# A sorted graph aggregation: other bucket counts per part, and merges and gathers begun at other times

## The chip, the core and the metric

One core of a Trainium2 chip runs the kernel. The metric is the device time of one execution in microseconds (us); the median of three runs of the kernel before was 1865.99 (1864.18 to 1870.74). The engines are named as in the profile: PE (matrix multiplication; PEld are its weight loads), DVE (vectors), ACT (activations and copies), POOL (here mostly the issue of indirect DMAs), SP (issue of other DMAs).

## What is computed

One layer of GraphSAGE on 12,500 nodes with 64 features and 800,000 random edges: features of the source nodes are summed for each destination node, scaled, and combined with the node's own features.

```
N, deg, D = 12500, 64, 64
E = N * deg
nsum = segment_sum(x[src], dst, N)       # 800,000 rows of 64 numbers, summed into 12,500
h_neigh = nsum * deg_inv[:, None]
return x @ w_self + h_neigh @ w_neigh
```

## The kernel before

The kernel never gathers the 800,000 rows. It sorts the edges into 7,546 buckets, one for each pair of 164 destination nodes and 128 source nodes, and turns each bucket into two small matrix products with one-hot matrices.

**Keys and sort (lines 249 to 284 and 427 to 464).** Each edge becomes one 32-bit key that holds bucket, half of the bucket, and the positions of source and destination. The keys stand in 128 partitions with 6,250 each. `sort_runs` sorts every partition by compare-exchange stages, a minimum and a maximum on DVE each; elements without a partner are copied by ACT. The last 30 stages are cut at `CUT` into three portions, so that the first part of the sorted run is done before the others.

**Parts, rows, runs.** The buckets are dealt to three parts. Part p has 128 rows with `KPRS[p]` buckets each (29, 20, 10), so part 0 holds buckets 0 to 3,711, part 1 the next 2,560, part 2 the rest. For each part a first gather (`find_rows`, `gather_runs`, lines 516 to 541) brings 16 pieces of the 128 sorted runs into each partition; DVE merges them to one (`merge_runs` over `LENA`, "first pass"); `split_rows` (543 to 570) stores the result, counts where rows begin, and gathers again, 8 pieces for each row; a second pass over `LENB` merges these to one sorted row a partition. `LENS` holds the lengths that are kept in each round. A round (`merge_round`, 300 to 334) begins with a minimum and a maximum (line 316), goes on with levels of the same kind (line 328), and lets ACT copy the elements that a level doesn't touch (line 312); the second level waits for that copy. The last round of part 0 (`merge_last`, 337 to 367) finishes the lower 1,770 elements of a row (`LOWER`) before the upper ones.

**Buckets.** `find_buckets` or `find_and_gather` count where each bucket's middle stands in its row, and a third gather by POOL brings a window of 200 elements a bucket into `v`. `decode_buckets` (766 to 855) splits the keys, four buckets a group: source positions go as bf16 to `sl` in DRAM, destination positions are transposed into `dlT`. What lies beyond the window's 128 elements is a leftover: found by MAX8 operations (857 to 863), collected by `leftovers` (865 to 922; `GRP` rows share one list), and later added by a matrix product of its own, from feature rows gathered by POOL into `lx` (`pick`, 989 to 1000; `HELD` = 5 buffers) and a one-hot (`spread`, line 1006).

**Node stage (`nodes`, 943 to 1090).** 944 tiles of eight buckets. For every 28 buckets SP loads their `sl` rows, spread over all partitions, into `slb` (line 933), and DVE makes the one-hots `ohs` (935) and `ohd` (940). PE multiplies the features by `ohs` into PSUM (966), ACT copies the result to `xg` (976; once the last part is decoded, DVE takes some of these, line 974), and PE multiplies `xg` by `ohd` and sums (1047). After every six destination blocks `finish` writes 984 nodes.

**What sets the order.** Everything from the end of the sort on is issued in an order written out by hand (`after_sort`, `sums_and_merge`, lines 1209 to 1385). The generators yield after each step: merges yield an estimate of their own DVE time in ns, side jobs yield the number of tiles to wait. Ahead of the node stage part 0 goes through alone; part 1's first pass (`merge`) fills in where part 0 waits: up to `WAIT` ns behind part 0's second gather, beside the counts, up to `BEHIND` ns, and beside the decode (1304 to 1309). In the node stage each tile adds `PACE[...] - spent` ns to a budget `t`, and merges are issued while it is positive; the first value of `PACE` that counts is for the time when part 1 is merged, the second for the time after. Part 1's second gather is a side job (`split`); its last yield is followed by the second pass of part 1, with part 2's first pass running meanwhile, and so on to part 2. A part's counts, gathers and decode (`change`, 1279) run one step a tile.

**Queues.** An engine takes its instructions in the order given, and so do the DMA queues of SP and POOL: a leftover gather on POOL whose buffer is still in use holds up the stores and gathers behind it.

Of the kernel before, what the change touches and what calls it, by code (L numbers as in the profile page):

```python
# [31 lines left out]
PITCH1 = 6400  # L32
KPRS = (29, 20, 10)
NP = len(KPRS)
# [6 lines left out]
NCNT = [(k + 3) // 4 for k in KPRS]  # L41
LENS = ((56, 92, 156, 280, 504, 936, 1776, 3424),
        (44, 72, 120, 208, 368, 676, 1264, 2412),
        (32, 48, 72, 124, 204, 368, 676, 1264))
SUP = 8
COUNTED = 4600
WAIT = 20e3
EARLY = 11e3
NSUP = 128 // SUP
LENA = [l[3:] for l in LENS]  # L50
LENB = [l[4:] for l in LENS]
PACE = (0, 420, 405)
LROW = [l[-1] for l in LENS]
LEAD = 616
EXT = 36
SIDE = H + EXT
PITCH2 = [l + 2 * SIDE for l in LROW]
PCS = (19, 13, 9)
PCSN = 14
PIECES = (12, 4)  # L60
GRP = (2, 4, 7)
CHK = [-(-128 // g) for g in GRP]
# [6 lines left out]
SIGMA = 6.0  # L69
LOWER = 1770  # L70
BEHIND = 5e3
NEARLY = 24
LAG = 4
HELD = 5
OCT = 6
OCTM = 256 // OCT + 1
# [223 lines left out]
def merge_round(nc, src, oth, off, other, rstride, nruns, ln, lout, late, filler=()):  # L300
# [18 lines left out]
    for j, (k, lo, *ends) in enumerate(plan):  # L319
        if not j and not late():  # L320
            both()
        for op, end, z in zip((OP.min, OP.max), ends, (1, 2 * k)):
            n = end - lo
# [7 lines left out]
            yield n2 * n / 0.96 + 125  # L331
        if not j:
            yield from islice(filler, 2)
        cur, nxt = nxt, cur


def merge_last(nc, src, oth, off, rstride, ln, lout, split, done):

# [10 lines left out]
    for a, e in alone:  # L349
        z = 2 * (a % ln) + a // ln  # L350
        nc.scalar.activation(at(src, z, e - a), at(oth, z, e - a), AF.Copy)
    edge = [split]
    for (first, *_), (then, *_) in zip(plan[-2::-1], plan[:0:-1]):
# [20 lines left out]
class Kernel:  # L374
# [168 lines left out]
    def split_rows(self, part, u, to, mps, queue):  # L543
# [20 lines left out]
        for j in range(SUP):  # L564
# [4 lines left out]
            yield 1  # L569
        yield 5  # L570

    def merge_runs(self, lens, u, pong, nruns, last=False):

# [5 lines left out]
        for ln, lout in zip(lens, lens[1:]):  # L579
            src, oth = bufs[par], bufs[1 - par]  # L580
            if last and nruns == 2:
                def done(rows):
                    assert rows is u
                    self.lower = True
                yield from merge_last(nc, src, oth, 0, rs, ln, lout, LOWER, done)
            else:
                for dt in merge_round(nc, src, oth, 0, 0, rs, nruns, ln, lout, lambda: self.late):
                    self.hold = dt < 0
                    yield abs(dt)
# [275 lines left out]
    def leftovers(self, part):  # L865
# [11 lines left out]
        for b in range(grp):  # L877
            nc.gpsimd.dma_start(many[:len(range(b, 128, grp)), b, :cand], found[b::grp])
        yield 8
        many = many.rearrange("p b i -> p (b i)")  # L880
# [62 lines left out]
    def nodes(self, pool, aps, mps):  # L943
# [6 lines left out]
        late = []  # L950
        done = []
        acc = None

# [35 lines left out]
        def pick(b0):  # L989
            if self.picked == len(done) or len([u for u in uses if u[5]]) >= HELD:  # L990
                return
# [19 lines left out]
        def add(u, stop=False):  # L1011
            o, _, _, f, e = u[:5]
            n = slice((f - o * OCT) * HN, (e - o * OCT) * HN)
            for h in range(2):
                nc.tensor.matmul(acc[h][:, n], u[5], u[7][:, h, n], start=False, stop=stop)  # L1015
# [193 lines left out]
    def after_sort(self, es, mps, aps):  # L1209
# [7 lines left out]
        with tc.manual_schedule():  # L1217
# [27 lines left out]
            rows = self.find_rows(2, mps)  # L1245
            for _ in self.merge_runs(LENA[0], u0, w0, NSUP):
                if rows and not self.hold and next(rows, None) is None:
# [5 lines left out]
            assert not rows  # L1253
            merge = self.merge_runs(LENA[1], u1, x, NSUP)
            t = 0
# [10 lines left out]
            n = t = 0  # L1266
            for dt in self.merge_runs(LENB[0], w0, u0, SUP, True):
                if self.lower:
# [18 lines left out]
    def sums_and_merge(self, es, mps, aps, x, u1, u2, u3, runs, first_two, va, vp, counts, merge):  # L1287
# [18 lines left out]
        for i, k in enumerate(self.decode_buckets(0, self.v, vp, mps)):  # L1306
            t += 1400 if i < 4 else 2800
            if k < KPRS[0]:
                t = fill(t) if t > 0 else t
        va.close()  # L1310
        first_two.close()
# [101 lines left out]
```

## Time and profile before

| What | Value |
|---|---|
| median of three runs | 1865.99 us |
| profiled execution, its own time | 1856.37 us |
| its span, first to last instruction | 1854.6 us |
| sort done, merges of part 0 begin | 437.6 us |
| second gather of part 0, second pass begins | 583 us, 605.7 us |
| first one-hots of the node stage | 803.4 us |
| first count of part 1, of part 2 | 1173 us, 1575 us |
| busy: DVE, ACT, PE, POOL | 93%, 60%, 53%, 31% |
| moved by DMA | 307.8 MB, 164 GB/s over the span |

The times are microseconds from the start of the span. A line of the timeline gives start, duration, engine, line, operation, written and read tiles, a count where several are put together, and in brackets how long the engine had stood idle and on what. In lines of groups the idle time and its causes stand behind the second bar. "f32 x2 ... 5.00" is two operations that took 5.00 us together. A matmul of line 966 is one bucket, so eight of them are a tile.

### The profile page before, as it was taken

What the parts mean: (1) busy time and instruction counts of PE and PEld (TensorE: products, weight loads), DVE (VectorE), ACT (ScalarE), POOL (GpSimd) and SP (SyncE); (2) the same over time, 40 slices, a digit from 0 to 9 for tenths busy, and PEclk for the clock granted to TensorE, in tenths of its full rate; (3) what the DMA queues carried; (4) which work ended last, traced back from release to release, by engine and by line L of the source; (5) the groups of instructions that cost most, each with busy time, mean ns of one, the idle gap of its engine ahead of it and who ended that gap; (6) DMA issues with size and microseconds to landing.
All of it is one profiled execution on the core that took longest, in us unless ns stands there. A gap on an engine that the chain in (4) does not pass through costs nothing.

```text
span 1854.6 us, 54153 instructions
## 1 busy us (share of the span) xinstructions
PE 986.6 (53%) x23413; PEld 851.9 (46%) x23413; DVE 1718.2 (93%) x1718; ACT 1116.7 (60%) x1587; POOL 576.2 (31%) x447
## 2 busy tenths in 40 slices
PE   3046000000000000058979979897898899888996
PEld 1015000000000000057868868776887788777885
DVE  6999999999999999989989999998898799978885
ACT  5263000113001005458979989899999899977885
POOL 2000000055502005404456535473332523532331
PEclk7567555555555555579989999999999999999998
DMA  5207100021002002169978888996889788977894
GB/s 174 54 0 169 39 0 0 38 79 51 18 4 73 10 0 82 47 216 266 274 249 253 251 248 254 296 282 227 264 250 284 234 265 242 326 200 257 274 268 118
DMA packets 176789, 307.79 MB, mean 166 GB/s; under 512 B 127885, under 2 KB 133596, under 8 KB 175772
## 3 DMA queue, kind: packets, MB, share of 16 engines
q1 hardware_dynamic: 98268, 275.58, 44.9%
q0 software_dynamic: 78272, 28.65, 9.6%
q8 instruction: 185, 3.03, 0.7%
q14 instruction: 64, 0.52, 0.1%
HBM read 277.01 MB, written 26.52 MB: 164 GB/s over the span
## 4 chain that ended last, share of the span: by engine, by line
DVE 19%; PE 13%; DMA 11%; issue 10%; SPq 5%; POOL 4%; ACT 4%; DVEq 0%; POOLq 0%; ACTq 0%
DMA slb<-sl 10%; PE ct L966 7%; DVE u L328 7%; PE acc L1047 5%; SPq L933 5%; DVE ohs L935 4%; DVE ohd L940 3%; ACT xg L976 2%; DVE u L362 2%; POOL u L565 1%; POOL lx L997 1%; POOL out L1123 1%; DVE u L316 1%; DMA sl<-l 1%; PE acc L1015 1%
## 5 line engine op out<-in xcount | busy, mean ns | idle before, releaser
L976 ACT ACTIVATE xg<-ct 128x1024 f16<-128x1024 f32 x919 | 862.6, 1074 | 104.4 <-PE ct L966 80.0
L966 PE MATMUL ct<-xh,ohs 128*128 128x128 f16 x7546 | 532.6, 224 | 87.9 <-DVE ohs L935 23.7
L966 PEld LDWEIGHTS <-ohs 128*128 128x128 f16 x7546 | 451.8, 100 | 125.4 <-issue 52.5
L328 DVE TENSOR_TENSOR u<-u 128x1512 f32<-128x1512 f32 (+57 forms) x316 | 425.7, 1362 | 12.9 <-ACT u L312 8.6
L1047 PE MATMUL acc<-ohd,xg 64*128 64x82 f16 x15092 | 395.2, 201 | 47.7 <-ACT xg L976 20.4
L1047 PEld LDWEIGHTS <-xg 64*128 64x128 f16 x15092 | 324.6, 96 | 104.6 <-issue 29.2
L997 POOL DMA_INDIRECT lx<-xt,ls x127 | 232.0, 1826 | 425.6 <-PE acc L1015 352.5
L940 DVE TENSOR_TENSOR ohd<-iota,dlT 128x2296 f16<-128x2296 bf16 x270 | 362.2, 1341 | 0.0
L935 DVE TENSOR_SCALAR ohs<-slb,pidx 128x3584 f16<-128x3584 bf16 x270 | 321.8, 1192 | 40.2 <-DMA slb<-sl 19.0
L509 PE MATMUL stp<-cx,swapa 128*128 128x16 f32 (+1 forms) x12 | 3.1, 335 | 398.0 <-DVE swapa L505 398.0
L260 DVE TENSOR_TENSOR a<-b 128x1040 f32<-128x1040 f32 (+41 forms) x130 | 194.7, 1539 | 3.5 <-DVE b L260 0.5
L260 DVE TENSOR_TENSOR b<-a 128x1040 f32<-128x1040 f32 (+46 forms) x150 | 194.6, 1345 | 3.2 <-ACT a L262 0.4
L538 POOL DMA_INDIRECT u<-d,ixa x48 | 72.5, 1511 | 390.8 <-ACT junka L526 335.4
L509 PEld LDWEIGHTS stp<-cx,swapa 128*128 128x128 f32 x12 | 2.6, 271 | 398.5 <-DVE swapa L505 398.5
L312 ACT ACTIVATE u<-u 128x256 f32<-128x256 f32 (+14 forms) x60 | 33.0, 618 | 170.6 <-DVE u L316 134.8
L1123 POOL DMA_DIRECT2D out<-o x27 | 99.1, 3800 | 103.1 <-ACT o L1117 89.8
L802 PE MATMUL tr<-idb,l 128*128 128x128 bf16 x59 | 7.6, 263 | 188.9 <-ACT l L796 188.9
L262 ACT ACTIVATE b<-a 128x2 f32<-128x2 f32 (+31 forms) x41 | 15.9, 402 | 127.1 <-DVE a L260 120.4
L802 PEld LDWEIGHTS <-l 128*128 128x128 bf16 x59 | 4.3, 114 | 191.2 <-ACT l L796 190.8
L316 DVE TENSOR_TENSOR u<-u 128x2016 f32<-128x2016 f32 (+11 forms) x40 | 61.9, 1563 | 16.2 <-DMA u<-da,ixb 8.8
L262 ACT ACTIVATE a<-b 128x1 f32<-128x1 f32 (+24 forms) x34 | 8.6, 259 | 105.4 <-DVE b L260 99.9
L565 POOL DMA_INDIRECT u<-da,ixb x24 | 36.9, 1539 | 88.6 <-ACT ixb L513 85.0
(158 smaller groups left out, 839.4 us busy)
## 6 DMA issues: line engine op xcount, KB each, us to landing
slb<-sl SPq DMA_DIRECT2D x1076, 224.0 KB
xt<-xh SPq DMA_DIRECT2D x1, 3136.0 KB
out<-o POOLq DMA_DIRECT2D x25, 123.0 KB
own<-os SPq DMA_DIRECT2D x12, 256.0 KB
out<-os SPq DMA_DIRECT2D x12, 256.0 KB
rd<-dst SPq DMA_DIRECT2D x5, 512.0 KB
rs<-src SPq DMA_DIRECT2D x5, 512.0 KB
lx<-xt,ls POOLq DMA_INDIRECT x127
```

The costliest lines, as they stand in the source:

```text
L260: nc.vector.tensor_tensor(view(dst, lo + sh, [[st, g], [1, l]]), x, y, op=op)
L316: nc.vector.tensor_tensor(at(oth, to, n), x, y, op=op)
L328: nc.vector.tensor_tensor(to, at(cur, ln + lo, n), at(cur, lo + k, n), op=op)
L538: nc.gpsimd.indirect_dma_start(out=u[:, i * w:(i + 1) * w], out_offset=None, in_=src, in_offset=bass.IndirectOffsetOnAxis(ap=self.start[pa ...
L933: nc.sync.dma_start(b[j::4], bass.AP(tensor=src.tensor, offset=src.offset, ap=[[0, 32], [1, n * 128]]))
L935: nc.vector.tensor_scalar(s.rearrange("p c s -> p (c s)"), b, self.pidx[:, :1], None, op0=OP.is_equal)
L940: nc.vector.tensor_tensor(d, self.iota[:, None].to_broadcast(wide), ix, op=OP.is_equal)
L966: nc.tensor.matmul(ct[:, i * 128:(i + 1) * 128], cols[i][0], self.xh[:, (b0 + i) % NB].rearrange("p a f -> p (a f)"), start=True, stop=True)
L976: nc.scalar.activation(xg[:, :cnt * 128], ct[:, :cnt * 128], AF.Copy)
L997: nc.gpsimd.indirect_dma_start(out=x, out_offset=None, in_=self.xt, in_offset=bass.IndirectOffsetOnAxis(ap=self.left[p][1][:, c:c + 1].bit ...
L1047: nc.tensor.matmul(acc[h][:, db % OCT * HN:(db % OCT + 1) * HN], xg[r, i * 128:(i + 1) * 128], d[r], start=db % OCT == 0 and sb == 0, stop ...
L1123: nc.gpsimd.dma_start(out, o[:n, at], accum_op=OP.add)
```

## The change

- The parts get 31, 20 and 8 buckets a row instead of 29, 20 and 10. `LENS` of parts 0 and 2, `LOWER`, the number of MAX8 pieces (`PCS`) and the rows that share a leftover list (`GRP` of part 2: 9 instead of 7) follow. Part 0 then ends at bucket 3,968, part 1 at 6,528.
- Part 1's first pass is handed to the merges of part 0 as a filler: in the rounds of the first pass from length 536 on, in all rounds of the second pass and in `merge_last`, one of its operations is issued between the first min/max pair and the second level. (Before, `filler` was there but empty.)
- `WAIT` is 22e3 instead of 20e3; after the decode of part 0 another 5e3 ns of part 1's merge are issued (`FIRST`).
- `PACE` is 328 and 362 instead of 420 and 405.
- The last yield of `split_rows` is 10 instead of 5: the merge behind a second gather begins five tiles later. The same for the wait of `leftovers` behind its copies: 10 instead of 8.
- `pick` counts a buffer as held for six tiles (`BACK`) after the product that reads it was issued.

```diff
-KPRS = (29, 20, 10)
+KPRS = (31, 20, 8)
-LENS = ((56, 92, 156, 280, 504, 936, 1776, 3424),
+LENS = ((60, 100, 168, 292, 536, 996, 1892, 3648),
         (44, 72, 120, 208, 368, 676, 1264, 2412),
-        (32, 48, 72, 124, 204, 368, 676, 1264))
+        (32, 44, 64, 108, 172, 308, 556, 1032))
-WAIT = 20e3
+WAIT = 22e3
-PACE = (0, 420, 405)
+PACE = (0, 328, 362)
-PCS = (19, 13, 9)
+PCS = (20, 13, 8)
-GRP = (2, 4, 7)
+GRP = (2, 4, 9)
-LOWER = 1770
+LOWER = 1890
+FIRST = 5e3
+BACK = 6
...
@@ merge_round @@
     for j, (k, lo, *ends) in enumerate(plan):
         if not j and not late():
             both()
+            yield from islice(filler, 1)
...
-        if not j:
-            yield from islice(filler, 2)
...
-def merge_last(nc, src, oth, off, rstride, ln, lout, split, done):
+def merge_last(nc, src, oth, off, rstride, ln, lout, split, done, filler=()):
...
         nc.scalar.activation(at(src, z, e - a), at(oth, z, e - a), AF.Copy)
+    yield from islice(filler, 1)
...
@@ split_rows @@
-        yield 5
+        yield 10
-    def merge_runs(self, lens, u, pong, nruns, last=False):
+    def merge_runs(self, lens, u, pong, nruns, last=False, filler=(), since=0):
...
-                for dt in merge_round(nc, src, oth, 0, 0, rs, nruns, ln, lout, lambda: self.late):
+                for dt in merge_round(nc, src, oth, 0, 0, rs, nruns, ln, lout, lambda: self.late,
+                                      filler if ln >= since else ()):
...
@@ leftovers @@
-        yield 8
+        yield 10
...
@@ nodes @@
+        added = []
...
-            if self.picked == len(done) or len([u for u in uses if u[5]]) >= HELD:
+            held = len([u for u in uses if u[5]]) + len([n for n in added if n > len(done) - BACK])
+            if self.picked == len(done) or held >= HELD:
                 return
...
@@ add @@
             o, _, _, f, e = u[:5]
+            added.append(len(done))
...
-            for _ in self.merge_runs(LENA[0], u0, w0, NSUP):
+            merge = self.merge_runs(LENA[1], u1, x, NSUP)
+            for _ in self.merge_runs(LENA[0], u0, w0, NSUP, filler=merge, since=LENA[0][1]):
...
-            merge = self.merge_runs(LENA[1], u1, x, NSUP)
...
-            for dt in self.merge_runs(LENB[0], w0, u0, SUP, True):
+            for dt in self.merge_runs(LENB[0], w0, u0, SUP, True, merge):
...
@@ sums_and_merge, after the decode of part 0 @@
+        fill(FIRST)
         va.close()
```

More of the change, by code (lines that the diff above doesn't have):

```diff
@@ L584, in done @@
                     self.lower = True
-                yield from merge_last(nc, src, oth, 0, rs, ln, lout, LOWER, done)
+                yield from merge_last(nc, src, oth, 0, rs, ln, lout, LOWER, done, filler)
             else:
-                for dt in merge_round(nc, src, oth, 0, 0, rs, nruns, ln, lout, lambda: self.late):
+                for dt in merge_round(nc, src, oth, 0, 0, rs, nruns, ln, lout, lambda: self.late,
+                                      filler if ln >= since else ()):
                     self.hold = dt < 0
```

## The prediction

> **What bounds the kernel now.** I read the page's totals first, then the busy time by stage, the rate of tiles, the waits, and last the timeline at each wait. The columns of the stage tables are stretch, length, then busy us (instructions) of PE, weight loads, DVE, ACT, POOL, then granted clock, DMA share, GB/s; the last four rows are the matmuls of line 966 alone.
>
> ```profile
> span 1854.6 us, 54153 instructions
> PE 986.6 (53%) x23413; PEld 851.9 (46%) x23413; DVE 1718.2 (93%) x1718; ACT 1116.7 (60%) x1587; POOL 576.2 (31%) x447
> 803.00:1633.00 830.00, 727.71 (x18284) 642.41 (x18285) 776.42 (x930) 764.86 (x990) 361.00 (x205) 0.96 0.86 262
> 953.00:1250.00 297.00, 262.79 (x6633) 231.79 (x6634) 291.93 (x314) 271.05 (x344) 152.16 (x70) 0.97 0.87 262
> 1350.00:1428.00 78.00, 70.05 (x1809) 61.76 (x1807) 75.11 (x83) 76.56 (x105) 25.86 (x11) 1.00 0.86 263
> 1633.00:1830.00 197.00, 174.48 (x4618) 157.74 (x4615) 173.98 (x208) 158.82 (x186) 56.92 (x34) 0.97 0.84 252
> 803.00:1170.00 367.00, 188.97 (x2639) 159.16 (x2640) 0.95 0.87 258
> 803.00:1575.00 772.00, 397.12 (x5581) 335.16 (x5582) 0.96 0.86 260
> 953.00:1250.00 297.00, 153.15 (x2167) 128.91 (x2168) 0.97 0.87 262
> 1350.00:1428.00 78.00, 41.27 (x601) 34.66 (x599) 1.00 0.86 263
> ```
>
> Up to 803 us (sorting, then merging and decoding part 0) DVE works almost alone; after it, the node stage runs 944 tiles of eight buckets, and DVE makes their one-hots and merges parts 1 and 2 between them. DVE's 93% is therefore two things. Before 803 every DVE microsecond is a microsecond of the kernel. In the node stage four limits stand close together. From 953 to 1250 DVE is at 291.93/297 = 98% and 2167/8 = 271 tiles take 1.096 us each: DVE's own work is 1.078 a tile, ACT's 271.05/271 = 1.00. From 1350 to 1428 DVE is at 96% and ACT at 98%: 75 tiles, 1.038 each. So taking work off DVE speeds a tile from 1.096 to about 1.04, and there ACT takes over. That is the number on which most hangs.
>
> ```profile
> DVE u L316 <- DMA u<-da,ixb: 8.8, 2, 7.3
> DVE u L328 <- ACT u L312: 8.6, 7, 2.6
> DVE u L316 <- DMA lx<-xt,ls: 7.0, 1, 7.0
> DVE ltop L860 <- DMA many<-top: 2.1, 2, 1.8
> POOL lx L997 <- PE acc L1015: 352.5, 74, 13.2
> 515.42 31.38 DVE L328 TENSOR_TENSOR u<-u 128x1282 f32<-128x1282 f32 x16 [1.64 <-ACT u L312]
> 605.70 4.42 DVE L316 TENSOR_TENSOR u<-u 128x2016 f32<-128x2016 f32 x2 [1.52 <-DMA u<-da,ixb]
> 612.68 31.20 DVE L328 TENSOR_TENSOR u<-u 128x836 f32<-128x836 f32 x16 [2.56 <-ACT u L312]
> 803.41 1.15 DVE L935 TENSOR_SCALAR ohs<-slb,pidx 128x3584 f16<-128x3584 bf16 x1 [6.22 <-DMA slb<-sl]
> 952.74 1.69 DVE L316 TENSOR_TENSOR u<-u 128x1472 f32<-128x1472 f32 x1 [7.25 <-DMA u<-da,ixb]
> 1456.61 1.93 DVE L316 TENSOR_TENSOR u<-u 128x816 f32<-128x816 f32 x2 [6.97 <-DMA lx<-xt,ls]
> ```
>
> A wait of DVE stands in brackets. These are the pauses that the edits touch: the copies of ACT inside merge rounds, the first one-hots after the decode, and the first merges behind the second gathers of parts 1 and 2 (952.74 and 1456.61; the second is put down to a leftover gather, the last thing on POOL's queue then).
>
> **The change part by part.** *Merges.* I wrote out the operations of merge_plan for both tables. All merges together have 453,028 elements a partition before and 453,500 after, with the same 376 operations: DVE saves nothing in sum. They move. Part 0 goes from 220,692 to 235,716 (+15,024), part 2 from 78,504 to 63,952 (-14,552). The price comes from two rows:
>
> ```profile
> 437.64 5.00 DVE L316 TENSOR_TENSOR u<-u 128x2240 f32<-128x2240 f32 x2
> 785.75 1.48 DVE L316 TENSOR_TENSOR u<-u 128x1264 f32<-128x1264 f32 x1
> 583.03 3.69 DVE L316 TENSOR_TENSOR u<-u 128x1664 f32<-128x1664 f32 x2
> 588.00 16.17 DVE L328 TENSOR_TENSOR u<-u 128x936 f32<-128x936 f32 x10
> ```
>
> (5.00/2 - 1.48)/(2240 - 1264) = 1.045 ns an element. Part 0's merges cost +15.7 us ahead of the node stage, uncovered; part 2's cost 15.2 us less inside it. The sort's portions shift by some 7 us of work from the last to the first, their sum stays.
>
> *Fillers.* Six merges of part 1 are put into part 0's later rounds, three in the first pass, three in the second: two of 3.69/2 = 1.85, one near 1.1, three near 1.6 (16.17/10), together 9.6 us. They cover pauses of 1.64, of 1.6 of the 2.56, and three small ones in the same places that are 1.5 together: 4.8. Net +4.8 before 803, but 9.6 us less to do after it.
>
> *WAIT, FIRST, counts.* WAIT adds 2 us of part 1 and covers the 1.52: +0.5. FIRST puts 5 us into the 6.22 gap, in which DVE waits for a load that doesn't need it: +0; without that cover it would cost 5. Two more windows in part 0 are gathered by POOL beside the decode; on DVE they cost one more merge in the count loop (1.6) and a larger search beyond the edges, about 0.9. Sum: the node stage begins 15.7 + 4.8 + 0.5 + 2.5 = **23.5 us later**.
>
> *What leaves the node stage on DVE:* the part 1 merges already done, 9.6 + 2 + 5 + 1.6 = 18.2; part 2's merges 15.2; two counts (1,996 elements), four leftover one-hots (127 become 123), one decode group:
>
> ```profile
> 1596.31 1.29 DVE L708 TENSOR_SCALAR_CACHE_REDUCE junk<-u,c 128x1046 bf16<-128x1046 f32 x1
> L1006 DVE TENSOR_SCALAR ohl<-wide,lp 128x164 f16<-128x164 f16 (+1 forms) x127 | 39.8, 320 | 0.0
> 1612.23 0.48 DVE L782 SCALAR_TENSOR_TENSOR w<-v,c 128x128 int32<-128x128 int32 x2
> L791 ACT ACTIVATE l<-w,edge 128x512 bf16<-128x512 int32 (+2 forms) x16 | 11.2, 700 | 23.3 <-DVE w L782 21.9 <-DMA sl<-l 1.4
> ```
>
> 1996 x 1.29/1046 = 2.5, 4 x 0.32 = 1.3, and 0.8. Together 38 us. PACE spreads what is left: 0.42 to 0.328 us a tile while part 1 is merged, 0.405 to 0.362 after. DVE's 1.078 a tile becomes 0.986, below ACT's 1.00. ACT loses one of its three decode groups of part 2 (four passes near 0.7, 2.8 us) and gains five small copies, about 1, since the column offset of part 2 is no longer 0.
>
> *The waits.* A second gather's merge now begins 25 tiles behind its first DVE step instead of 20. These rows time both splits:
>
> ```profile
> 923.47 0.28 DVE L505 TENSOR_TENSOR swapa<-accb,cx 128x128 f32<-128x128 f32 x1
> 931.11 1.24 POOL L565 DMA_INDIRECT u<-da,ixb  x1 [9.89 <-ACT ixb L513]
> 934.62 1.24 POOL L565 DMA_INDIRECT u<-da,ixb  x1 [0.31 <-issue]
> 936.23 1.61 POOL L565 DMA_INDIRECT u<-da,ixb  x1 [0.16 <-issue]
> 938.20 5.24 POOL L565 DMA_INDIRECT u<-da,ixb  x1 [0.16 <-issue]
> 943.79 2.53 POOL L565 DMA_INDIRECT u<-da,ixb  x1 [0.16 <-issue]
> 946.68 0.95 POOL L565 DMA_INDIRECT u<-da,ixb  x1 [0.16 <-issue]
> 949.29 3.37 DMA u<-da,ixb
> 1429.15 0.28 DVE L505 TENSOR_TENSOR swapa<-accb,cx 128x128 f32<-128x128 f32 x1
> 1434.16 1.49 POOL L997 DMA_INDIRECT lx<-xt,ls  x1 [13.20 <-PE acc L1015]
> 1438.64 1.65 POOL L565 DMA_INDIRECT u<-da,ixb  x1 [0.30 <-ACT ixb L513]
> ```
>
> Split 1: DVE would reach the merge at 923.5 + 25 x 1.04 = 949.5, the data are there at 949.29 + 3.37 = 952.7. So 3 of the 7.25 us remain: -4.2. Split 2: 1429.2 + 26 = 1455.2 against 1456.6, and POOL's 13.2 us stand before the leftover gather is gone, some 2 us earlier: about -5 (bounds 5 and 7). Nothing else fails to run: during split 1 part 2's first merges fill in.
>
> The Trainium skill's page "SBUF — State Buffer", section "Who interferes with whom", speaks against this: DVE and GpSimd share a pair of ports, an operation of DVE in a two-port mode holds it whole, and descriptors issued on POOL wait. The trace agrees: the five gathers made while DVE ran took 1.24 to 5.24, those made while it stood still 0.95. By that rule the wait of split 1 would stay near 7 us; it is one of the rivals below.
>
> *BACK.* Leftover gathers come out once their buffer has been free for 6 tiles. POOL's 352.5 us of standing are off the path except for what queues behind (row 1434.16). The gather itself moves by 6.5 - 352.5/74, under 2 us, and is used 10 tiles after it at the earliest: 0. The ends are a gain of the 2 us counted above and a loss of a few us where PE comes first. *leftovers:* two more tiles cover 1.8 + 0.3, though part 2 has nine copies there instead of seven: -1.
>
> **Sum.** Tiles 0 to 330 (803 to 1170): 20 us of start and the 7.25 aside, 312 tiles in 340 us, 1.089 each; at 1.04 they take 324.5: -15.5, and -4.2. Tiles 330 to 698 (to 1575, 405 us): PACE takes 0.043 x 368 = 16 off DVE, of which I take half, since ACT is as full: -8, and -5. Part 2's counts and decode: -3. Leftovers: -1. The node stage shrinks by 36.7, of which 23.5 are lost ahead of it: **-13 us**. The profiled execution took 1856.4 (its span 1854.6 and 1.8 around it), 9.6 under the median of the runs; I set the 13 against the median: 1853.
>
> **Rivals.**
> - *DVE was the only limit* (1836). All 38 us come back, and the waits of 7.25, 6.97 and 1.8: 54 - 23.5 = -30. For it: 98% busy. Against it: the stretch at 1350, where ACT was fuller than DVE, and 1.038 was the best that was reached.
> - *The second gathers stay late* (1859). With a DVE that no longer stands still, the last three gathers of split 1 take the mean of the first five, (1.24 + 1.24 + 1.61 + 5.24 + 2.53)/5 = 2.4, instead of 0.95: the data come 4.3 us later. At split 2 it is 3 x (1.65 - 0.95) = 2.1. So 6 of the 13 us go. For it: 5.24 against 0.95 in one series. Against it: 1.65 at the other split is mild. This is what the Trainium skill's page "SBUF — State Buffer", section "Who interferes with whom", would lead to.
> - *A quarter of the relief* (1866). The pace per tile falls to about 1.08: 9.5 + 13 of waits and decode, against 23.5: nothing to see.
> - *ACT already sets the tile* (1876, slower). One mechanism, in the tiles before part 1 is merged: ACT's evictions of 1.00 us, with their waits for PE, keep the tile at 1.09 whatever DVE does. Only the 13 us come back, +10. It decides if the 748 tiles that took 830 us (1.11 each) stay above (830 - 23.5)/748 = 1.078. Against it: DVE had only 2% of slack there, ACT 9%.
>
> **How the numbers follow.** Forecast 0.44, DVE alone 0.18, late gathers 0.10, a quarter 0.15, ACT 0.13. A measurement of this kernel can tell about 0.3%, 5.6 us, from no change: faster means under 1860.4. Forecast 9 in 10 of its chance, DVE alone whole, late gathers 6 in 10: 0.64 faster. The quarter and the rests: 0.21 the same; 0.15 slower. The forecast's own range is 1843 to 1862. The whole range, 1834 to 1876, leaves out the better half of the DVE case and the worse half of the ACT case.
>
> **What would show it.** The first one-hots of the node stage near 827 instead of 803.41; the stretch 200 to 400 us after them at 1.04 us a tile with DVE below 97% and ACT above 95%; waits before line 316 of about 3 and 1 us; POOL's line of 352.5 under 100. I am wrong if the node stage starts before 820, or if its pace before part 1 is merged stays above 1.075 or falls below 1.02.

## The result and the profile after

The changed kernel takes **1880.72 us** (median of 4 runs, 1878.57 to 1883.72) against 1867.24 for the kernel before (median of 4): ratio 1.0082, 95% interval 1.0062 to 1.0101. It is slower, by 13.5 us; the forecast was 13 us faster than the median. The profiled execution took 1878.57 us.

The page's totals of the changed kernel:

```profile
span 1876.8 us, 54147 instructions
PE 1003.8 (53%) x23405; PEld 858.9 (46%) x23405; DVE 1714.5 (91%) x1702; ACT 1122.2 (60%) x1594; POOL 542.6 (29%) x446
```

DVE's total is nearly the same as before (1718.2), as it had to be: its work was moved, not removed. What was moved shows by stage. The next rows are windows of the changed kernel, with the columns of the prediction's tables; the first two are the prediction's two stretches, each 24 us later, the third is 983 to 1191 us (tiles 140 to 340), and the last two are the matmuls of line 970 (line 966 before) alone.

```profile
977.00:1274.00 297.00, 268.23 (x6718) 235.47 (x6716) 278.00 (x289) 272.60 (x337) 120.39 (x63) 0.96 0.88 269
1374.00:1452.00 78.00, 74.68 (x1938) 66.32 (x1932) 75.16 (x86) 77.17 (x96) 22.35 (x12) 1.00 0.90 279
983.00:1191.00 208.00, 189.31 (x4906) 167.82 (x4900) 202.52 (x189) 197.12 (x238) 79.86 (x35) 0.98 0.89 268
977.00:1274.00 297.00, 155.18 (x2190) 0.96 0.88 269
983.00:1191.00 208.00, 109.87 (x1592) 0.98 0.89 268
```

From 983 to 1191 us 1592/8 = 199 tiles take 1.045 us each, with DVE at 97% and ACT at 95%. That is the pace forecast. In the wider stretch, which runs on into part 1's counts, 2190/8 = 274 tiles take 1.085 us each, and DVE has fallen from 98% to 278.00/297 = 94%: that is above the 1.075 that the prediction set as a sign of being wrong, though for the tiles before part 1 is merged. The stretch that it named, 200 to 400 us after the first one-hots (1027 to 1227 us), has 1520/8 = 190 tiles in 200 us, 1.053 each, with DVE at 96% and ACT at 93%. Next the timeline of the changed kernel at the places that the prediction named, and the waits of DVE and POOL in its node stage (engine, line, what it waited for; us in total, times, longest):

```profile
827.61 1.15 DVE L938 TENSOR_SCALAR ohs<-slb,pidx 128x3584 f16<-128x3584 bf16 x1 [0.72 <-issue]
904.11 0.29 DVE L507 TENSOR_TENSOR swapa<-accb,cx 128x128 f32<-128x128 f32 x1 [2.07 <-ACT junkb L555]
917.14 1.53 POOL L567 DMA_INDIRECT u<-da,ixb  x1 [9.91 <-ACT g L1060]
937.29 1.69 DVE L318 TENSOR_TENSOR u<-u 128x1472 f32<-128x1472 f32 x1 [5.56 <-DMA lx<-xt,ls]
1328.34 4.77 POOL L1129 DMA_DIRECT2D out<-o  x1 [2.67 <-ACT o L1123]
1335.05 2.85 POOL L881 DMA_DIRECT2D many<-top  x4 [0.29 <-POOL many L877]
1349.10 1.10 DVE L863 MAX8 ltop<-many 32x8 f32<-32x40 f32 x8 [9.82 <-DMA many<-top]
1678.13 0.76 DVE L785 SCALAR_TENSOR_TENSOR w<-v,c 128x256 int32<-128x256 int32 x2 [7.60 <-DMA v<-d,ix]
DVE ohs L938 <- PE ct L970: 44.5, 35, 4.9
DVE ohs L938 <- remote: 12.0, 2, 8.7
POOL lx L1002 <- PE acc L1021: 336.0, 63, 12.1
```

The node stage begins at 827.61 us (826.9 forecast), and the 6.22 us gap ahead of it is gone. Behind the second gather of part 1 the wait of 7.25 us is still 5.56, the one behind that of part 2 has gone, and two new ones of 9.82 and 7.60 us have come. DVE's largest waits are now for TensorE: 44.5 us before the one-hots of line 938 (18.9 before those of line 935 in the kernel before).

### The profile page after: what moved, and what is told of

It reads as the page before. It is cut to its first block, busy times and chain, and to the rows that moved or that the text cites. A ratio compares the mean times of both kernels' runs of the same rounds, so it can differ in the third digit from the quotient of the medians.

```text
span 1876.8 us, 54147 instructions
## 1 busy us (share of the span) xinstructions
PE 1003.8 (53%) x23405; PEld 858.9 (46%) x23405; DVE 1714.5 (91%) x1702; ACT 1122.2 (60%) x1594; POOL 542.6 (29%) x446
## 3 DMA queue, kind: packets, MB, share of 16 engines
q8 instruction: 185, 3.03, 0.6%
## 5 line engine op out<-in xcount | busy, mean ns | idle before, releaser
L1053 PE MATMUL acc<-ohd,xg 64*128 64x82 f16 x15092 | 407.2, 202 | 50.6 <-issue 27.2
L331 DVE TENSOR_TENSOR u<-u 128x1402 f32<-128x1402 f32 (+55 forms) x316 | 423.9, 1359 | 10.9 <-ACT u L314 6.7
L938 DVE TENSOR_SCALAR ohs<-slb,pidx 128x3584 f16<-128x3584 bf16 x270 | 323.4, 1198 | 67.5 <-PE ct L970 44.5
L1053 PEld LDWEIGHTS <-xg 64*128 64x128 f16 x15092 | 329.1, 96 | 113.6 <-issue 43.9
L1002 POOL DMA_INDIRECT lx<-xt,ls x123 | 207.9, 1691 | 444.7 <-PE acc L1021 336.0
L262 DVE TENSOR_TENSOR a<-b 128x1050 f32<-128x1050 f32 (+41 forms) x130 | 194.8, 1540 | 3.6 <-ACT b L264 0.6
L262 DVE TENSOR_TENSOR b<-a 128x1032 f32<-128x1032 f32 (+46 forms) x150 | 194.6, 1346 | 3.2 <-ACT a L264 0.4
L264 ACT ACTIVATE b<-a 128x2 f32<-128x2 f32 (+31 forms) x41 | 15.9, 401 | 121.3 <-DVE a L262 114.2
L318 DVE TENSOR_TENSOR u<-u 128x2144 f32<-128x2144 f32 (+11 forms) x40 | 61.8, 1557 | 6.2 <-DMA lx<-xt,ls 5.6
L567 POOL DMA_INDIRECT u<-da,ixb x24 | 30.1, 1255 | 111.6 <-ACT ixb L515 98.0
```

The lines of the kernel that those rows point to most:

```text
L262: nc.vector.tensor_tensor(view(dst, lo + sh, [[st, g], [1, l]]), x, y, op=op)
L318: nc.vector.tensor_tensor(at(oth, to, n), x, y, op=op)
L331: nc.vector.tensor_tensor(to, at(cur, ln + lo, n), at(cur, lo + k, n), op=op)
L938: nc.vector.tensor_scalar(s.rearrange("p c s -> p (c s)"), b, self.pidx[:, :1], None, op0=OP.is_equal)
L1002: nc.gpsimd.indirect_dma_start(out=x, out_offset=None, in_=self.xt, in_offset=bass.IndirectOffsetOnAxis(ap=self.left[p][1][:, c:c + 1].bit ...
L1053: nc.tensor.matmul(acc[h][:, db % OCT * HN:(db % OCT + 1) * HN], xg[r, i * 128:(i + 1) * 128], d[r], start=db % OCT == 0 and sb == 0, stop ...
```

## The experiments

They ran on five chips, called A to E; kernels on one chip share its runs of the kernel before (A 1869.51 us, median of 17; B 1869.91, of 9; C 1860.50, of 31; D 1869.15, of 23; E 1859.18, of 11). Ratios are to the kernel before on the same chip, with 95% intervals. Tiles are read from the matmuls of line 966/970, starts from the first one-hots.

**Is the trace typical, and which group of edits costs? (chip A)** `again` is the changed kernel itself. `sched` has all edits but the new bucket counts and PACE; `parts` has only the new bucket counts; `pace_old` has all edits but PACE.

```diff
 # sched: the changed kernel, with             # parts: the kernel before, with
-KPRS = (31, 20, 8)                            -KPRS = (29, 20, 10)
+KPRS = (29, 20, 10)                           +KPRS = (31, 20, 8)
-PACE = (0, 328, 362)                          # and LENS, PCS, GRP, LOWER to match
+PACE = (0, 420, 405)
 # pace_old: the changed kernel, with
-PACE = (0, 328, 362)
+PACE = (0, 420, 405)
```

> The changed kernel unaltered, once more, for a second profile. Two theories. Standing pauses: PE's stretches of few matmuls per us that the profile puts down to nothing (43.4 us of 'issue' before PE in the node stage, against 23.5 in the kernel before) and the slow tiles 20-100, 400-480, 600-620, 800-840 belong to the program's order, and return at the same tiles within a few us. Chance pauses: they come from where other traffic happens to be, and this profile has them at other tiles, with the same sum to within 10 us. Time 1879 to 1883 by both.

> The schedule's edits alone (fillers, WAIT, FIRST, later merges behind second gathers, BACK), with the parts (29, 20, 10) and the PACE of before. Theory A, ACT sets the tile: the node stage begins near 809 (fillers 4.8, WAIT 0.5) instead of 803.4, and wins back only the waits in front of the merges, 10 us: ratio to before 0.997 (0.993 to 1.000). Theory B, relief is converted but lost again in new pauses of PE: some 18 us of merging leave the node stage, of which half would come back if no new pauses appear: ratio 0.990 (0.985 to 0.996); with new pauses of 10 us or more, 0.996 to 1.003, and PE's 'issue' idle is above 33 us.

> The parts (31, 20, 8) alone, with what follows from them (LENS, LOWER, PCS, GRP), and the schedule and PACE of before. Both theories: the node stage begins near 821 (15.7 for the larger merges, 2.5 for counts and decode). Theory A: the node stage wins only the shorter decode of part 2, 3 us: ratio 1.008 (1.006 to 1.011). Theory B: 20 us of DVE work leave it and half come back unless new pauses eat them: ratio 1.003 (0.999 to 1.006).

> The changed kernel with PACE (0, 420, 405) again. Theory A: no difference, ratio to before 1.008 (1.006 to 1.010). Theory C, the lower PACE is the fault: it leaves DVE idle early (19 to 22 of 25 us from 875 to 950) and puts the merging, part 2's decode and the time from which DVE shares in the evictions some 30 tiles later: then merges end near tile 750 again, and the ratio falls to 1.000 (0.995 to 1.004).

Measured: again 1883.86 (one run). From tile 340 on it loses at the same tiles as the first trace; ahead of that it lies up to 12 us further behind, and TensorE's unexplained idle time is 56 us instead of 43. sched 1.0043 (1.0023 to 1.0064), parts 1.0077 (1.0045 to 1.0109), pace_old 1.0123 (1.0091 to 1.0155). So the two halves add up (0.43 + 0.77 = 1.20%), both lose, and the lower PACE is worth 0.4 to 0.5% to the good. `sched` and `pace_old` lie outside the ranges of both their theories, `parts` in that of theory A (ACT sets the tile). In `parts` the first one-hots come 18.3 us later (821.68 against 803.41 us), as much as the 15.7 and 2.5 expected, and the median is 14.65 us higher. So taking 15 us of part 2's merges out of the node stage gave about 4 us back; by the interval of the ratio it can be anything from none to 10.

**What is a microsecond of DVE worth, and what do the loads cost? (chip B)** `before_again` is the kernel before. `before_light` takes 37 us of DVE out of its node stage evenly. The two `noslb` kernels load the source positions only for the first three blocks.

```diff
 # before_light
-            nc.vector.tensor_scalar(s..., b, ...)            # 28 buckets
+            m = min(n, 27)
+            nc.vector.tensor_scalar(s[:, :m]..., b[:, :m * 128], ...)
-            nc.vector.tensor_tensor(d, ...)                  # 14 pairs
+            nc.vector.tensor_tensor(d[:, :m // 2], ...)
 # before_noslb, after_noslb
...                                                  # the first three buffers are kept
-            for j in range(4):
+            for j in range(4 if c < 3 * 28 else 0):
                 nc.sync.dma_start(b[j::4], ...)
```

> The kernel before, once more, unchanged. Its first profile (1856.4 us) lay 9 us under the median of the timed runs, and in it TensorE stood only 23 us in the node stage for no reason that the profile shows (issue), against 43 and 56 us in two profiles of the changed kernel. Theory 'a lucky profile': this one takes 1863 to 1873 us, the node stage (from 803 us on) 1060 to 1068 instead of 1051, and TensorE's unexplained idle time is 30 to 45 us; then part of the pauses that looked new in the changed kernel are those of any run. Theory 'the pauses come with the change': 1855 to 1862 us, unexplained idle time under 28 us.

> The kernel before, with DVE work taken from the node stage evenly: of every 28 buckets the last source one-hot and the last two destination one-hots are not made, others are read in their place (left out: 1/28 of the source one-hots, 1/14 of the destination ones; matrix products, loads and the order stay). That is 270 x (1198/28 + 1343/14) ns = 37 us of DVE, as much as the change took from there. Theory 'relief of DVE comes back nearly whole' (what the prediction's pace of 1.04 us a tile said): 30 to 37 us less than the kernel before, about 1832 to 1840 us. Theory 'the other engines and the loads hold the pace, whatever DVE does': 8 to 15 us less, 1853 to 1861 us. In the first case the change loses its gain by where it puts its work; in the second there was little to gain.

> The kernel before, with the source positions of the buckets loaded only for the first 84 buckets, and those read again for all others (left out: about 99% of the loads into slb, 240 MB, so that the sums are of wrong rows; every engine's work stays). With it the loads no longer share the DMA engines with the gathers, the stores and TensorE's own instruction fetches, and no one-hot waits for its load. Theory 'the loads are a limit of the tile': the node stage shrinks by 25 us or more. Theory 'they are hidden': within 8 us of the kernel before. Unexplained idle time of TensorE: under 8 us if it is a fetch that the loads hold up, 20 us or more if it is not.

> The changed kernel, with the same left out. Theory 'TensorE's instruction fetch loses against dense loads, and the change makes such stretches denser': the clusters of unexplained idle time (43 us) go to under 10, and with them the changed kernel beats the kernel before without these loads by the 13 us that the prediction had. Theory 'the runs of gathers on POOL do it, whatever the loads': the clusters stay where POOL issues gathers back to back (near 865, 1245, 1267, 1502 us), 20 us or more in sum. Theory 'no engine gains from less DVE work': no clusters, and still 8 us or more slower than the kernel before without these loads.

Measured: before_again 1882.50 (one run), above what either theory expected and above all nine other runs of this kernel on the chip (up to 1875.87), so its gaps may be larger than usual. before_light 0.9944 (0.9925 to 0.9964), 0.56% or 10.5 us (7 to 14 by the interval) for 37 us of DVE. before_noslb 0.9782 (0.9761 to 0.9803), 41 us less; after_noslb 0.9880 (0.9855 to 0.9905).

The loads are a limit of the tile. But they don't explain the change: without them the changed kernel is still 0.9880/0.9782 = 1.0100 of the kernel before.

before_again also showed that the first profile of the kernel before isn't like the others. Here are the waits of TensorE for which the profile has no cause ("issue"), first of that first profile, then of before_again, then of before_noslb:

```profile
PE acc L1047 <- issue: 11.4, 15, 1.8
PE ct L966 <- issue: 10.1, 13, 1.9
```

```profile
PE acc L1047 <- issue: 26.3, 46, 1.6
PE ct L966 <- issue: 22.3, 35, 2.2
```

```profile
PE acc L1050 <- issue: 9.0, 19, 1.2
PE ct L969 <- issue: 4.4, 13, 0.5
```

In the node stage that makes 23, 50 and 13 us; the 13 lie between the two values expected. The gaps are of two kinds: single ones of up to 2.2 us, and clusters (three or more within 2.5 us of each other). before_again has 31 us in single gaps or pairs and 19 in 6 clusters, before_noslb 3 and 10, after_noslb 3 and 18: without the loads the single gaps go, while clusters remain. A cluster looks like this (timeline of the changed kernel; TensorE first, then the other engines at its end):

```profile
1502.23 0.45 PE L970 MATMUL ct<-xh,ohs 128*128 128x128 f16 x5 [0.33 <-issue]
1502.96 0.26 PE L1053 MATMUL acc<-ohd,xg 64*128 64x82 f16 x4 [0.29 <-issue]
1503.68 0.20 PE L1053 MATMUL acc<-ohd,xg 64*128 64x82 f16 x1 [0.46 <-issue]
1504.39 0.33 PE L1053 MATMUL acc<-ohd,xg 64*128 64x82 f16 x4 [0.52 <-issue]
1505.83 0.32 PE L1053 MATMUL acc<-ohd,xg 64*128 64x82 f16 x4 [1.11 <-issue]
1506.56 0.22 PE L1053 MATMUL acc<-ohd,xg 64*128 64x82 f16 x1 [0.41 <-issue]
1507.27 0.81 PE L1053 MATMUL acc<-ohd,xg 64*128 64x82 f16 x18 [0.48 <-issue]
1507.36 1.95 DVE L938 TENSOR_SCALAR ohs<-slb,pidx 128x3584 f16<-128x3584 bf16 x1 [8.73 <-remote]
1507.42 1.94 ACT L980 ACTIVATE xg<-ct 128x1024 f16<-128x1024 f32 x2 [5.63 <-remote]
```

For five microseconds TensorE gets one to four products at a time, 0.72 us apart (once 1.44), and DVE, idle for some 3 us already (8.73 in all), and ACT (5.63) stand until it is over.

**Does any one engine set the tile? Does BACK cost? (chip C)** `before_lightact` lets ACT copy 984 of 1024 columns of each tile, `before_lightpe` leaves out the summing products of every eleventh bucket; each was meant to take 36 to 39 us from one engine. `back0` is the changed kernel without BACK, `parts_pace` the new bucket counts with a lower PACE.

```diff
 # before_lightact
-   nc.scalar.activation(xg[:, :cnt * 128], ct[:, :cnt * 128], AF.Copy)
+   nc.scalar.activation(xg[:, :cnt * 128 - 40], ct[:, :cnt * 128 - 40], AF.Copy)
...                                   # the last bucket's product reads 40 columns earlier
 # before_lightpe
+   if (b0 + i) % 11 == 5 and (db % OCT or sb): continue
 # back0                      # parts_pace: as parts, and
-BACK = 6                     -PACE = (0, 420, 405)
+BACK = 0                     +PACE = (0, 360, 362)
```

> The kernel before, with work taken evenly from ACT in the node stage: each of its 919 evictions copies 984 of 1024 columns (left out: the last 40 columns of a tile; the last bucket's product reads columns that overlap its neighbour's). 919 x 1074 ns x 40/1024 = 39 us of ACT. The same amount taken from DVE gave 8 us (0.9944). Theory 'ACT sets the tile': 28 to 39 us less than the kernel before. Theory 'no one engine sets it; the tile is the sum of short waits of each for the other': 5 to 15 us less, as with DVE. Theory 'ACT has slack': under 4.

> The kernel before, with work taken evenly from TensorE: the two summing products of every eleventh bucket are left out (686 of 7546; their share of the sum is missing). 395 us / 11 = 36 us of TensorE, and 6% of its instructions. Theory 'TensorE sets the tile (it waits least often for others)': 28 to 40 us less than the kernel before. Theory 'no one engine sets it': 5 to 15 us less. Theory 'TensorE has slack': under 4.

> The changed kernel with BACK at 0: a leftover buffer counts as free as soon as its product was issued, as in the kernel before. Theory 'BACK lets POOL run its leftover gathers in bursts, and TensorE trickles beside a burst': 5 to 12 us less than the changed kernel (1869 to 1876 us), with fewer clusters of unexplained idle time at leftover gathers. Theory of the prediction 'BACK is worth nothing or 2 us to the good': 1880 to 1884 us. Rival 'without it the gathers of rows queue behind a waiting leftover gather again': 5 us or more over the changed kernel.

> The kernel before with the new bucket counts and a lower PACE (360 and 362; 328 would end the merges after their rows are needed), none of the other edits. With the old PACE the new bucket counts took 1884 us. With all edits the lower PACE was worth 15 us (1895 to 1881). Theory 'a lower PACE spreads the merges and is the one edit that helps; the other edits of the schedule cost some 10 us': 1868 to 1876 us. Theory 'the lower PACE only mends what the other edits do': 1880 to 1888 us.

Measured: before_lightact 0.9981 (0.9957 to 1.0004), before_lightpe 0.9960 (0.9940 to 0.9979). By the totals of the pages the three thinned kernels have 34 us less of DVE (1718.2 to 1684.5), 27 less of ACT (1116.7 to 1089.3) and 13 less of TensorE (986.6 to 973.2, where the ends of matmuls are modelled). They gave 0.56% (10.5 us, chip B), 0.19% (3.5 us) and 0.40% (7.4 us, both chip C). None of it came back nearly whole, so no one engine sets the tile. ACT's 3.5 us are within noise of nothing and under the 4 that stood for slack, and the three rates can't be ranked, since chip B shows clusters and chip C none. back0 0.9999 (0.9977 to 1.0021), parts_pace 1.0041 (1.0014 to 1.0067); the latter has no counterpart on its chip, since `parts` ran on chip A. back0 looked as if BACK cost the whole 0.8%. But no profile of chip C has a single cluster, and the kernel before is 9 us faster there.

**BACK or the chip? (chip D)** `again_b` and `back0_b` are the changed kernel with BACK 6 and 0, `before_back` is the kernel before with BACK = 6, and `old_parts` has the schedule edits alone, with BACK 0, PACE (0, 380, 385) and the old bucket counts.

```diff
 # before_back, in the kernel before
+   held = len([u for u in uses if u[5]]) + len([n for n in added if n > len(done) - BACK])
-   if self.picked == len(done) or len([u for u in uses if u[5]]) >= HELD:
+   if self.picked == len(done) or held >= HELD:
```

> The changed kernel, unchanged, beside the next three on one chip. Theory 'the change loses by itself': 0.6 to 1.0% over the kernel before, as in the first comparison. Theory 'part of the loss was the chip': the runs so far fell on chips where every kernel, the one before too, showed clusters of unexplained idle time of TensorE, or none (kernel before: 1869.5 and 1869.9 us with clusters, 1860.5 without); then the ratio depends on which kind this chip is: near 1.000 to 1.003 without clusters, 1.006 to 1.010 with them.

> The changed kernel with BACK at 0, which took 0.9999 of the kernel before on a chip without clusters. Theory 'BACK is the edit that costs, 0.8% or 15 us': 12 to 18 us less than the changed kernel on this same chip, and 0.998 to 1.002 of the kernel before. Theory 'BACK is worth nothing, as predicted, and the difference was the chip': within 4 us of the changed kernel. Between them, 4 to 12 us: BACK has a share.

> The kernel before with BACK = 6 alone. Theory 'BACK is the edit that costs': 8 to 16 us over the kernel before (1.004 to 1.009). Theory 'worth nothing': 0.998 to 1.002.

> The changed kernel with the bucket counts of before (29, 20, 10), with BACK at 0 and PACE at 380 and 385: the fillers, WAIT, FIRST and the later merges alone. The node stage then starts some 2 us later than before instead of 24, with 18 us of DVE less to do in it. Theory 'the fillers help and part 0's size is what they have to pay for': 0.994 to 0.998 of the kernel before, faster than both kernels. Theory 'a microsecond of DVE in the node stage is worth a quarter': 18/4 - 2 = 2 to 3 us less, 0.998 to 1.000. Theory 'the later merges cost': over 1.002.

Measured: again_b 1.0077 (1.0050 to 1.0105), back0_b 1.0070 (1.0043 to 1.0097), before_back 1.0017 (1.0001 to 1.0032), old_parts 1.0010 (0.9989 to 1.0030). BACK is worth next to nothing here (on chip C the changed kernel was not run with BACK 6), and the same kernel that is 0.9999 on chip C is 1.0070 on chip D. All four profiles of D have 8 to 11 clusters. old_parts, without the larger part 0, is level with the kernel before: the fillers give no gain either.

before_back and again_b are the best pair to see where the gain went: one chip, clusters in both, both profiles 6 to 7 us under their medians. These are windows of the node stage from its first one-hots to the first product of tile 943, the last, cut at the first product of tile 340; first of before_back, then of again_b:

```profile
803.05:1177.42 374.37, 330.32 (x8300) 290.55 (x8300) 362.21 (x391) 339.90 (x416) 169.69 (x80) 0.96 0.87 262
1177.42:1843.61 666.19, 587.37 (x14760) 515.92 (x14757) 594.96 (x752) 590.26 (x764) 255.85 (x158) 0.97 0.84 254
```

```profile
827.64:1187.29 359.65, 328.31 (x8294) 289.82 (x8294) 334.79 (x358) 336.71 (x412) 146.31 (x78) 0.97 0.88 270
1187.29:1857.81 670.52, 594.07 (x14757) 521.67 (x14753) 579.78 (x754) 592.38 (x769) 238.55 (x155) 0.96 0.83 252
```

In the first part DVE has 362.21 - 334.79 = 27.4 us less to do, and the part is 14.7 us shorter. In the second DVE has 15.2 us less to do, and the part takes 4.3 us more: DVE is idle for 91 us instead of 71. Together 42.6 us of DVE gave 10.4. The same cut on the kernel before (its first profile) and back0, which have no clusters:

```profile
803.41:1180.53 377.12, 329.16 (x8300) 291.60 (x8300) 363.40 (x391) 339.11 (x415) 168.18 (x82) 0.95 0.87 260
1180.53:1836.60 656.07, 578.99 (x14760) 513.92 (x14757) 591.93 (x753) 588.80 (x765) 249.74 (x156) 0.97 0.84 258
```

```profile
827.45:1188.68 361.23, 324.87 (x8293) 286.91 (x8294) 333.44 (x359) 337.37 (x412) 153.51 (x78) 0.97 0.89 268
1188.68:1834.30 645.62, 579.09 (x14756) 514.02 (x14753) 579.35 (x753) 589.06 (x768) 244.35 (x155) 0.97 0.86 263
```

Here the first part gives 15.9 us for 30.0 of DVE, the second 10.5 for 12.6: 26.3 in all, 2 more than the later start takes. So the pairs differ in the second part: with clusters nothing came back there, without them most. These are single executions, and the chip of the kernel before's first profile is not known. With back0_b in place of again_b, on chip D, the first part gives 6.0 us and the second 0.7.

**Do runs of gathers cause the clusters? (chip E)** Clusters stood beside three and more gathers of POOL in a row. `before_spaced` sets the gathers of the kernel before apart; `after_nolx` takes most leftover gathers from the changed kernel.

```diff
 # before_spaced: behind each gather of leftovers, rows (parts 1, 2) and windows
+   self.pause(6)
 # after_nolx: five buffers, filled once
+   if fresh:
        nc.gpsimd.indirect_dma_start(out=x, ...)
```

> The kernel before with six short memsets on POOL (0.2 us each) behind every gather of the node stage, of leftovers, rows and windows; behind rows there was one, behind the others none. No two gathers then start less than about 2.3 us apart, instead of 1.3. On chips with clusters TensorE trickles (about four products every 0.72 us) beside runs of three and more gathers. Theory 'runs of gathers make TensorE trickle': no clusters of three and more gaps are left, unexplained idle time of TensorE is under 30 us instead of 45 to 50, and the kernel takes 4 to 10 us less than before (0.995 to 0.998). Theory 'the gathers only run fast because the other engines have stopped': clusters as before, 45 us or more, and 0 to 6 us more time, since rows and windows come later. If the kernel before shows no clusters on this chip, nothing is decided on this point.

> The changed kernel with leftover gathers for the first five lists only; their buffers are read again for all others (left out: 118 of 123 gathers of leftover rows, so that their sums are of wrong rows). Theory 'runs of gathers make TensorE trickle': the clusters at leftover gathers alone (near 1362 to 1372 and 1726 to 1730 us) are gone, the one near 866 stays (its five gathers are the first), the others get shorter since no leftover gather stands between the gathers of rows and windows; the kernel takes 4 to 12 us less than the changed kernel, 1.001 to 1.005 of the kernel before. Theory 'the gathers are not the cause': clusters at the same places, and within 3 us of the changed kernel (1.006 to 1.009).

Measured: before_spaced 1.0364 (1.0346 to 1.0383), after_nolx 0.9940 (0.9923 to 0.9957). Neither decides the question, since chip E shows no clusters in either profile: what causes them stays open. Both kernels were built to have fewer runs of gathers; that the chip itself shows no clusters rests on the time of the kernel before, 1859.18 us as on chip C, and on after_nolx, whose trace has none at its first five gathers, where the changed kernel has one on chips A and D. Both say something else. The leftover gathers may cost some 11 us: the changed kernel with them and BACK 0 was 0.9999 on chip C, but a comparison across two chips doesn't show it. And POOL is not off the path in a decode. before_spaced was expected to lose 6 us at most; of the 72 us that its trace lies behind at its end, 38 come between tiles 380 and 420 and 26 between 700 and 740, where the windows are gathered and POOL also issues the stores that the decode waits for (waits of before_spaced):

```profile
ACT l L797 <- DMA sl<-l: 49.3, 2, 32.0
DVE w L783 <- ACT l L793: 27.9, 1, 27.9
DVE w L783 <- DMA v<-d,ix: 24.0, 4, 8.4
```

## Why the prediction was wrong

**What bounds the kernel.** The prediction took DVE's 98% from 953 to 1250 us, most of it ahead of part 1's first count, as the state of the stage. There its reading held. The kernel before has these rows for tiles 140 to 340, all engines and then the matmuls of line 966:

```profile
964.25:1180.53 216.28, 192.56 (x4920) 170.34 (x4917) 214.50 (x206) 200.07 (x242) 104.01 (x39) 0.98 0.86 257
964.25:1180.53 216.28, 112.78 (x1604) 0.98 0.86 257
```

DVE is at 99%, and the 200 tiles go from 216.3 us to 208.7 in the changed kernel, 1.04 a tile as forecast, with DVE at 97% (200 to 204 us in again, again_b, back0 and back0_b). From tile 340 to the end it did not hold: on average the kernel before has DVE at 591.93/656.07 = 90%, ACT at 90%, TensorE at 88% there. DVE is full in stretches of that part (99% from 1462 to 1540 us) and idle in others. The prediction quoted a row of it (1633 to 1830, DVE 88%) and did not draw the conclusion; the stretch it took as the limit (1350 to 1428 us, DVE 96%, ACT 98%) is among its fullest.

**The step that failed** is the second half of the sum: "PACE takes 0.043 x 368 = 16 off DVE, of which I take half, since ACT is as full: -8, and -5", with "Part 2's counts and decode: -3. Leftovers: -1". That is -17 for the tiles from 330 on. Behind tile 340 the pair on chip D gave +4.3, with 15.2 us of DVE taken away and the wait of split 2 (6.6 us in before_back) gone: what DVE was relieved of became idle time, 91 us instead of 71. With back0_b in place of again_b it is -0.7. The pair without clusters gave -10.5. `parts` points the same way, with a wide interval: part 2's merges, 15.2 us, returned about 4. before_light, thinned evenly over the whole stage, says it in general: 37 us of DVE are worth 10.5 us, 28%. Why so little comes back on the chips with clusters stays open.

**The first half** was over-sized too, by less: -15.5 and -4.2 were forecast up to tile 330; measured up to tile 340 were -14.7 on chip D (-6.0 by back0_b) and -15.9 without clusters. With both, the sum of the node stage on chip D is -10.4 instead of -36.7. Against the start, 24.6 us later there, that leaves +14.2, the result on that chip (1883.42 - 1869.15 = 14.3).

**The later start** was right in its sum and its main parts: 23.5 forecast, 24.2 measured (827.61 - 803.41); the larger part 0 alone 15.7 + 2.5, against 18.3 in `parts`. FIRST was free as predicted: the first one-hots waited 0.72 us.

**DVE's work** that leaves the node stage was 38 us by the sum; the windows on chip D show 42.6, of which some 6 are five evictions of the last tiles (line 974/978, 1.22 us each) that ACT did instead. The amount was right, its worth was not.

**The waits.** Split 2's is gone, as forecast (before_again doesn't have it either). Split 1's stayed at 5.56 where 3 was forecast. DVE came to it 27.6 us behind its first step (26 forecast), but the first gather left POOL 13.0 us behind that step (904.11 to 917.14) instead of 7.6, and its row was 33.2 us behind it instead of 29.3. The "leftovers" term had the wrong sign: the four copies of part 1 now stand on POOL behind a store of `out` (rows 1328.34 and 1335.05), and DVE waits 9.82 us where all such waits were 2.1 before. It waits 5.0 us in again and 6.0 in again_b, and not at all with BACK 0 (back0, back0_b). The wait of 7.60 us in part 2's decode was not foreseen at all. But these waits don't decide the time: back0, level with the kernel before on chip C, still has 6.9 us at split 1 and 10.0 at split 2.

By the Trainium skill's page "SBUF — State Buffer", section "Who interferes with whom", as the prediction read it, split 1's wait would have stayed near 7 us because gathers issued beside a busy DVE take longer. The wait stayed near that, but mostly for another reason: the first gather started 5.4 us later behind DVE's first step, while the eight took 11.5 us together, none over 1.86, where the kernel before had 14.7 and one of 5.24.

**BACK** was rightly put at nothing (1.0017 and 1.0077 against 1.0070). But "POOL's line of 352.5 under 100" was wrong: it is 336.0 us. Outside the decodes POOL has little else to do (busy for 29% of the span), so it is ahead and stands somewhere; the line says nothing about time.

**The rivals.** The side of the result was that of "ACT already sets the tile" (1876), but not its mechanism: the tile did fall to 1.04 where it said 1.09, and 27 us off ACT gave 0.19%, within noise of nothing. "A quarter of the relief" (1866) had the rate of chip D right (10.4 of 42.6) and failed on the 13 us of waits and decode, which it still counted whole; without them it would give 1867 + 23.5 - 9.5 = 1881.

**The profile that was read.** It lay 9.6 us under the median, which the prediction set aside as an offset. It has no clusters, like those of chips C and E; the changed kernel's first profile has nine. On chips A, B and D every profile has them. By the medians the changed kernel gave back some 10 us of its later start on chip D, and with BACK 0 all 24 on chip C. That the freed DVE has more to wait for where TensorE itself is held up fits the waits of line 938 (for TensorE 21.0 us in back0, 38 to 48 in the three profiles of the changed kernel, 22 and 35 in before_back and before_again), but this is argued, not shown.

## What to carry to other kernels

Before a relief is priced, read the idle time of the relieved engine in every stage. Where it is already idle for a tenth, what it is relieved of may only add to its idle time, and an experiment that thins the engine evenly tells the rate (here 28% for DVE on chip B). Work moved from such a stage to one where an engine runs alone was paid in full at its new place and returned at a lower rate. And a kernel's profile should be taken more than once, on more than one chip, before its gaps are put down to its own order.

## What the runs showed of the hardware

- Chips differ in more than speed. On A, B and D the profiles have 17 to 32 us in clusters where TensorE gets one to four products every 0.72 us (10 and 18 without the loads), always beside gathers issued by POOL, mostly three or more in a row. On C, with the same runs of gathers, there are none, nor on E, whose two kernels have fewer. The kernel before takes 1869 to 1870 us on the former, 1859 to 1861 on the latter. The cause is open.
- The dense loads cost TensorE single gaps of up to 2.2 us: 9 to 31 us a run with the loads, 3 in both kernels without them. The queue that brings instructions moved 3.03 MB in 185 packets in the changed kernel, 16.4 KB each:

```profile
q8 instruction: 185, 3.03, 0.6%
```

The Trainium skill's page "Runtime: NRT & Kernel Launch", section "Instruction fetch mechanics", has an engine's instructions arrive in blocks of 16 KiB; the packets agree. It calls the cost of these fetches mostly hidden; that the single gaps are fetches held up by the loads would fit, but no run here shows it.
